# Widening steps moved behind the second layer, and the token transposes ahead of it, in the expert stage of a fused mLSTM, mixture-of-experts and MLP kernel

## The chip, the cores and the metric

The kernel runs on one core of a Trainium2 chip. The metric is the device time of one execution in microseconds (us), the median of several runs. The engines are named as the profile names them: PE (TensorE, matrix products), PEld (its weight loads), DVE (VectorE), ACT (ScalarE), POOL (GpSimd) and SP (SyncE, which issues most transfers here).

## What is computed

Three layers follow each other: a recurrent attention (mLSTM) over 4 sequences of 768 positions, a mixture of 8 experts of which each of the 3072 tokens uses one (`e_idx`, the largest of its 8 gate logits; `gate_w` is that gate's softmax), and a dense two-layer MLP. The expert layers are 320 -> 1024 -> 320, the MLP's 320 -> 2048 -> 320.

```python
def _moe_ref(x, w_gate, w_output_gate, w1, w2) -> np.ndarray:
...
    eom = 1.0 / (1.0 + np.exp(-(x @ w_output_gate)))
...
    for e in range(E):
        mask = e_idx == e
...
        h = np.maximum(x[mask] @ w1[e], 0.0)
        ye = h @ w2[e]
        out[mask] = gate_w[mask, None] * eom[mask, e, None] * ye
...
def _moe2_ref(x, w_in, w_out) -> np.ndarray:
    h = x @ w_in
    g = np.maximum(0.01 * h, h)
    return (g @ w_out).astype(np.float32)
```

The MLP's weights arrive as float64 and are rounded to float32 on the chip, from pairs of 32-bit words. That rounding is called widening here.

## The kernel before

Every large product is made in three parts: each operand is split into a rounded high part and a low part, and high times high, high times low and low times high are added up in one PSUM bank. PSUM has 8 banks that are given out in turn, so a new tile waits until the tile eight before it has been read.

After the attention, experts are worked on one after the other. Expert 0 is the first one; the others are ordered by falling token count and are called places 1 to 7. Places 1 to 3 have room for 512 tokens, places 4 to 7 for 384. One place does this:

- **First layer** (`Expert.one`, L989): 8 steps f = 0 to 7, each of 8 products (L954) into one PSUM tile `ph`, then `gh` by ACT (relu, L1004) and `gl` by DVE (what the rounding left, L1005).
- **Second layer** (`Expert.out`, L1008): one step per 128 tokens, 24 products each (L963 to L965: for every f two with `gh` and one with `gl`), then ACT scales the result (`yo`, L1019) and POOL writes it out by an indirect transfer (L1025).
- **Next tokens**: at f = 0 POOL issues the gathers of the next place's rows into `xr` (L978, one per 128 tokens); after f = 4 DVE copies the last 64 columns of them a second time (`dup`, L896); PE transposes them in three groups (`px`, L903, one group per 128 columns; the third group holds the copied columns), and ACT and DVE split them into `xh` and `xl` (L930 to L934).
- **Next weights**: seven parts are split, each by an ACT cast (`w1h`, `w2h`, L878) and a subtraction on DVE or POOL (`w1l`, `w2l`, L879). The loads of the weights after those are issued from SP when a raw buffer has been read (L783 to L791).
- **Widening**: a piece of 128 x 1024 numbers takes seven steps (L807 to L832): `size` (L809), `bound` (L813), `shift` (L816), `sign` (L819), `power` (L823) and `rest` (L827) on DVE, then `finish` (L831) on POOL and a transfer out. `rest` also lets ACT issue the load of a further piece. Places 1 to 3 do two pieces each, places 4 to 6 one, place 7 none; one more piece is done during the attention.

Within a stage the order of the instructions on PE, ACT, DVE and POOL is the order in which the program calls them. Two tables of closures set it (L1260 to L1284): `plan[f]` is called after step f of the first layer, `late[j]` after step j of the second. Before, `plan` holds the splits and the first four steps of the first piece, `late` the rest:

```python
for f in range(FE // P):
    gs.append(ex.one(wts[e], xs, f, e))
    ...
    for act in plan[f]:
        act()
for j in range(nj):
    ex.out(wts[e], gs, m, j, e)
    if j == 0 and tk:
        tk.turn()
        xs = tk.split()
    for act in late[j]:
        act()
```

Of the kernel before, what the change touches and what calls it, by code (L numbers as in the profile page):

```python
# [19 lines left out]
P = 128  # L20
# [34 lines left out]
def apart(tc, inst, before, why):  # L55
    """Writes of distinct rows of one tensor need not wait for each other."""
    for p in before:
        tc.declare_no_dep(inst.ins, p.ins, reason=why)
    before.append(inst)


def keep_warm(nc, psum, t, n):
    """Products nobody reads, so that the tensor engine's clock stays up over a wait."""
    pt = psum.tile([P, 512], F32, tag="ps", name="warm")
    for _ in range(n):
        nc.tensor.matmul(pt, t[:, 0:P], t[:, 0:512], start=True, stop=True)  # L66
# [8 lines left out]
def attention(ctx, tc, qT, kT, k, v, i_gate, f_gate, o_gate, psum, ident, router, side, feed, fill):  # L75
# [62 lines left out]

    # constants
    resetm = apool.tile([BH, NC_, P], F32, name="resetm")  # L140
# [4 lines left out]
    for j in range(3):  # L145
        nc.gpsimd.affine_select(
            sel, sel, pattern=[[-1, BH]], compare_op=ALU.not_equal, fill=1.0, base=-BH * j, channel_multiplier=1
        )
    # gate scans
    m = apool.tile([BH, S], F32, name="m")  # L150
# [8 lines left out]
    def gates(c0, c1, eng):  # L159
        """Steps that work out the gate factors of chunks c0 to c1 - 1."""  # L160
        n = c1 - c0
# [340 lines left out]
class Router:  # L502
# [54 lines left out]
    def clear(self):  # L557
        """Steps that give the slot table and the rows of xd that are written last their first contents."""
        put = self.nc.sync.dma_start
        late = lambda b: self.xd[b * S + (NC_ - 2) * P : (b + 1) * S].rearrange("(t p) e -> p t e", p=P)  # L560
        return [lambda: put(self.slots.rearrange("(p r) w -> p r w", p=P), self.init)] + [
            lambda b=b: put(late(b), self.zero[:, None, :].to_broadcast([P, 2, DM])) for b in range(B)
        ]
# [26 lines left out]
    def span(self, c, b):  # L590
        """Tiles routed together: a whole chunk, or one tile of the last chunk."""
        if c == NC_ - 1:
            return {B // 2 - 1: (0, B // 2), B - 1: (B // 2, B // 2)}.get(b, (0, 0))
        return (0, B) if b == B - 1 else (0, 0)
# [96 lines left out]
class Order:  # L691
    """Experts 1 to E - 1 in order of falling token counts, and the tiles of P slots past each one's share."""

# [32 lines left out]
    def expert(self):  # L726
        """Registers that hold the experts of places 1 to E - 1."""
        n = E - 1
        self.nc.gpsimd.tensor_copy(self.perm, self.key[:, 0:n])
        _, regs = self.nc.values_load_multi_w_load_instructions(  # L730
            self.perm[0:1, 0:n], engines=SP_ACT, min_val=1, max_val=n
        )
        return (0, *regs)

    def past(self, pool):
        """Steps that list the tiles of P slots past each expert's share."""
        v = self.nc.vector
# [57 lines left out]
def widen(nc, tile, dma, add, src, dst):  # L795
    """float64 bits (pairs of int32) rounded to float32, in small steps."""
    n = src.shape[1] // 2
    st = {}
    v = nc.vector

    def load():
        raw = tile("raw", 2 * n)
        dma.dma_start(raw, src)
        raw = raw.rearrange("p (n t) -> p n t", t=2)
        st["lo"], st["hi"] = raw[:, :, 0], raw[:, :, 1]

    def size():  # L807
        u = st["u"] = tile("u", n)
        v.tensor_scalar(u, st["hi"], 0x7FFFFFFF, None, ALU.bitwise_and)  # L809

    def bound():
        uf = st["u"].bitcast(F32)
        v.tensor_scalar(uf, uf, MIN64, MAX64, ALU.max, ALU.min)  # L813

    def shift():
        v.tensor_scalar(st["u"], st["u"], 3, (1 << 30) - 1, ALU.logical_shift_left, ALU.bitwise_and)  # L816

    def sign():
        v.scalar_tensor_tensor(st["u"], st["hi"], -(1 << 30), st["u"], ALU.bitwise_and, ALU.bitwise_or)  # L819

    def power():
        p = st["p"] = tile("p", n)
        v.tensor_scalar(p, st["u"], -(1 << 23), None, ALU.bitwise_and)  # L823

    def rest():
        r = st["r"] = tile("r", n).bitcast(F32)
        v.scalar_tensor_tensor(r, st["lo"].bitcast(U32), 2.0**-52, st["p"].bitcast(F32), ALU.mult, ALU.mult)  # L827

    def finish():
        uf = st["u"].bitcast(F32)  # L830
        add.tensor_add(uf, uf, st["r"])  # L831
        nc.sync.dma_start(dst, uf)  # L832

    return load, [size, bound, shift, sign, power, rest, finish]


class Weights:
    """One expert's weights as high and low parts, made in small steps."""

# [9 lines left out]
    def loads(self):  # L849
        """Steps that load both matrices, part by part."""  # L850
        a, b = self.src
        r1 = self.r1 = self.stage.tile([P, 3, FE], F32, tag="r1", name="r1")
        r2 = self.r2 = self.stage.tile([P, FE // P, DM], F32, tag="r2", name="r2")
        put = self.nc.sync.dma_start
        ones = [
            lambda: put(r1[:, 0], a[0:P]),
            lambda: put(r1[:, 1], a[P : 2 * P]),
            lambda: (put(r1[0:64, 2], a[2 * P :]), put(r1[64:P, 2], a[2 * P :])),
        ]
        b = b.rearrange("(f p) d -> p f d", p=P)  # L860
        return ones + [lambda f=slice(i, i + 2): put(r2[:, f], b[:, f]) for i in range(0, FE // P, 2)]

    def split1(self, t, eng):
        if t == 0:
            self.w1h = self.slot.tile([P, 3, FE], F32R, tag="w1h", name="w1h")
            self.w1l = self.slot.tile([P, 3, FE], F32R, tag="w1l", name="w1l")
        self.split(self.r1[:, t], self.w1h[:, t], self.w1l[:, t], eng)

    def split2(self, i, eng):
        nf = FE // P  # L870
        if i == 0:
            self.w2h = self.slot.tile([P, nf, DM], F32R, tag="w2h", name="w2h")
            self.w2l = self.slot.tile([P, nf, DM], F32R, tag="w2l", name="w2l")
        f = slice(2 * i, 2 * i + 2)
        self.split(self.r2[:, f], self.w2h[:, f], self.w2l[:, f], eng)

    def split(self, raw, hi, lo, eng):
        self.nc.scalar.copy(hi, raw)  # L878
        eng.tensor_sub(lo, raw, hi.bitcast(F32))  # L879

    def steps(self, engs):
# [5 lines left out]
class Tokens:  # L887
    """Token rows, turned to have features on the partitions and split in high and low parts."""

# [18 lines left out]
    def pieces(self):  # L908
        """Steps that turn the rows by blocks of 32 x 32 on the vector engine."""
        n, blocks = self.n, self.xr.rearrange("p j (g f) -> p j g f", f=32)  # L910
# [126 lines left out]
class Fill:  # L1037
    """The first slots of expert 0, worked on while the last tokens are routed."""

# [16 lines left out]
    def up(self, n):  # L1056
        """Products of n parts of the first layer."""
        for _ in range(n):
# [14 lines left out]
def overflow_tile(nc, pool, ex, slots, w1, w2, e, row):  # L1073
    """Tokens of expert e in the P slots from `row` on, all in float32."""
    psum, ident = ex.psum, ex.ident
# [27 lines left out]
def mlstm_moe_mlp(  # L1103
# [94 lines left out]
    with ExitStack() as mctx:  # L1198
# [19 lines left out]
        for e in range(E):  # L1218
# [25 lines left out]
            if e == 0:  # L1244
# [13 lines left out]
                ]  # L1258
            else:
                plan = [  # L1260
                    [w_(0, 0)],
                    [s1(nxt, 0, V)],
                    [s1(nxt, 1, G), w_(0, 1)],
                    [s1(nxt, 2, V), lambda: nx2.load1()],
                    [w_(0, 2), s2(nxt, 0, G), lambda: tk and tk.dup()],
                    [s2(nxt, 1, V)],
                    [s2(nxt, 2, G), w_(0, 3)],
                    [],
                ]
                late = [  # L1270
                    [s2(nxt, 3, V), lambda: nx2.load2(), w_(0, 4)],
                    [w_(0, 5, 6)],
                    [],
                    [],
                ]
                if nw == 2:
                    late[1] += [w_(1, 0, 1)]
                    late[2] += [w_(1, 2, 3, 4)]
                    late[3] += [w_(1, 5, 6)]
                if e < 4:  # L1280
                    late[1].append(past[e - 1])
                if e == E - 1:
                    plan[6], plan[7] = [s2(nxt, 2, G), s2(nxt, 3, V)], [lambda: nx2.load2()]
                    late = [[s1(nx2, 0, V)], [s1(nx2, 1, V)], [s1(nx2, 2, V)]]  # L1284
# [3 lines left out]
            for f in range(FE // P):  # L1288
# [3 lines left out]
                for act in plan[f]:  # L1292
                    act()
            for j in range(nj):
                ex.out(wts[e], gs, m, j, e)
                if j == 0 and tk:
                    tk.turn()
# [90 lines left out]
def _laid_out(inputs):  # L1388
    """q and k with positions innermost; k, v (and a one for each head) and o_gate as token rows of all heads."""
    import numpy as np  # L1390
# [35 lines left out]
```

## Time and profile before

| what | value |
|---|---|
| median of 3 runs | 796.43 us (796.18 to 798.04) |
| the profiled execution, first to last instruction | 798.3 us |
| PE busy in it | 745.3 us, 93% |
| DVE, POOL, ACT busy | 504.0 us, 383.1 us, 337.1 us |
| places 1 to 7 of the expert stage | 223.88 us to 440.68 us |

The profiled execution's span stands for its whole time; it lies 1.9 us above the median and 0.3 us above the slowest of the three runs. Busy time is a mean over stages with different limits; the expert stage has to be read by its own windows. A row of the timeline gives the start, the duration, the engine, the source line, the operation, what it writes and reads, and in brackets how long the engine had been idle and for what. Durations of instructions that follow each other overlap a little, because the next one starts before the last has drained.

### The profile page before, as it was taken

What the parts mean: (1) busy time and instruction counts of PE and PEld (TensorE: products, weight loads), DVE (VectorE), ACT (ScalarE), POOL (GpSimd) and SP (SyncE); (2) the same over time, 40 slices, a digit from 0 to 9 for tenths busy, and PEclk for the clock granted to TensorE, in tenths of its full rate; (3) what the DMA queues carried; (4) which work ended last, traced back from release to release, by engine and by line L of the source; (5) the groups of instructions that cost most, each with busy time, mean ns of one, the idle gap of its engine ahead of it and who ended that gap; (6) DMA issues with size and microseconds to landing.
All of it is one profiled execution on the core that took longest, in us unless ns stands there. A gap on an engine that the chain in (4) does not pass through costs nothing. (4 is left out here: it accounts for less than half of the span.)

```text
span 798.3 us, 14570 instructions
## 1 busy us (share of the span) xinstructions
PE 745.3 (93%) x5450; PEld 691.7 (87%) x5450; DVE 504.0 (63%) x956; ACT 337.1 (42%) x726; POOL 383.1 (48%) x408
## 2 busy tenths in 40 slices
PE   8778888899898998979989899999999999999998
PEld 6778888888788787978989898998998998998998
DVE  8889999977368988986575575606507417317120
ACT  5476545432353525334426535405416316226141
POOL 8556775554564836546535235506407307217131
PEclk9898897799998999889999999999999999999999
DMA  6885785410786655645655201100100100100000
GB/s 180 241 240 133 207 215 127 134 52 20 212 296 207 217 200 183 248 131 183 202 151 171 83 11 41 42 25 1 41 25 1 46 22 1 34 18 0 17 18 16
DMA packets 61790, 87.68 MB, mean 110 GB/s; under 512 B 8396, under 2 KB 53464, under 8 KB 60440
## 3 DMA queue, kind: packets, MB, share of 16 engines
q1 hardware_dynamic: 55928, 67.43, 28.6%
q10 hardware_dynamic: 2336, 10.75, 3.7%
q0 software_dynamic: 3456, 8.58, 3.4%
q8 instruction: 43, 0.70, 0.4%
q14 instruction: 27, 0.22, 0.1%
HBM read 67.87 MB, written 19.51 MB: 109 GB/s over the span
## 5 line engine op out<-in xcount | busy, mean ns | idle before, releaser
L1343 POOL TENSOR_TENSOR g2l<-lk,g2h 128x512 fp32r<-128x512 f32 (+1 forms) x112 | 126.7, 1134 | 213.8 <-ACT g2h L1342 203.7
L1352 DVE TENSOR_TENSOR lk<-p,lk 128x512 f32<-128x512 f32 (+1 forms) x112 | 69.0, 616 | 180.9 <-ACT lk L1351 179.0
L954 PE MATMUL p<-xhm,w1h 128*128 128x512 f32 (+1 forms) x336 | 119.7, 360 | 0.0
L954 PE MATMUL p<-xhm,w1l 128*128 128x512 f32 (+1 forms) x336 | 119.2, 359 | 0.0
L965 PE MATMUL po<-w2h,g2l 128*128 128x320 f32 x384 | 118.7, 309 | 0.0
L964 PE MATMUL po<-w2l,g2h 128*128 128x320 f32 x384 | 118.7, 309 | 0.0
L963 PE MATMUL po<-w2h,g2h 128*128 128x320 f32 x384 | 118.6, 309 | 0.0
L1351 ACT ACTIVATE lk<-p 128x512 f32<-128x512 f32 (+1 forms) x112 | 60.2, 538 | 73.5 <-PE p L954 73.5
L965 PE MATMUL po<-w2h,gl 128*128 128x320 f32 x208 | 69.8, 336 | 19.2 <-DVE gl L1005 19.2
L954 PE MATMUL p<-xlm,w1h 128*128 128x512 f32 (+1 forms) x224 | 80.6, 360 | 0.0
L963 PEld LDWEIGHTS po<-w2h,g2h 128*128 128x128 f32 x384 | 72.1, 188 | 0.2
L964 PEld LDWEIGHTS po<-w2l,g2h 128*128 128x128 f32 x384 | 72.1, 188 | 0.2
L965 PEld LDWEIGHTS po<-w2h,g2l 128*128 128x128 f32 x384 | 72.1, 188 | 0.0
L954 PEld LDWEIGHTS p<-xhm,w1h 128*128 128x128 f32 x336 | 63.6, 189 | 9.4 <-DVE xhm L934 0.2
L954 PEld LDWEIGHTS p<-xhm,w1l 128*128 128x128 f32 x336 | 63.4, 189 | 9.4
L963 PE MATMUL po<-w2h,gh 128*128 128x320 f32 x208 | 68.3, 328 | 0.0
L1025 POOL DMA_INDIRECT x<-yo,ms x26 | 28.1, 1080 | 80.9 <-ACT yo L1019 79.6
L964 PE MATMUL po<-w2l,gh 128*128 128x320 f32 x208 | 66.8, 321 | 0.0
L1366 ACT COPY yo<-po 128x320 f32<-128x320 f32 x24 | 10.2, 426 | 130.7 <-PE po L965 130.7
L965 PEld LDWEIGHTS po<-w2h,gl 128*128 128x128 f32 x208 | 41.8, 201 | 24.9 <-DVE gl L1005 24.9
L1342 ACT CAST g2h<-lk 128x512 fp32r<-128x512 f32 (+1 forms) x112 | 61.7, 551 | 1.6 <-DVE lk L1352 1.6
L916 DVE STREAM_TRANSPOSE xtm<-x2r 32x384 f32<-32x384 f32 (+3 forms) x144 | 59.6, 414 | 2.8
(245 smaller groups left out, 1703.7 us busy)
## 6 DMA issues: line engine op xcount, KB each, us to landing
r<-in_moe_w_dram SPq DMA_DIRECT2D x6, 1280.0 KB
r<-in_moe_w_dram SPq DMA_DIRECT2D x7, 1024.0 KB
raw<-in_moe_w_out_dram ACTq DMA_DIRECT2D x5, 1024.0 KB
r<-in_moe_w_dram SPq DMA_DIRECT2D x16, 256.0 KB
raw<-in_moe_w_in_dram ACTq DMA_DIRECT2D x4, 1024.0 KB
v<-in_v_dram SPq DMA_DIRECT2D x24, 164.0 KB
o<-in_o_gate_dram SPq DMA_DIRECT2D x6, 640.0 KB
k<-in_k_dram SPq DMA_DIRECT2D x24, 160.0 KB
```

Of the source, the lines that this page charges most:

```text
L916: self.nc.vector.transpose(out=xt[f, k].rearrange("p k (j t) -> p k j t", t=P)[:, :, :, t], in_=blocks[t, :, g].rearrange("p j k f -> p k ...
L954: nc.tensor.matmul(ps, a, b, start=(i == 0), stop=(i == len(seq) - 1))
L963: nc.tensor.matmul(ps, gh[:, js], wh, start=(f == 0), stop=False)
L964: nc.tensor.matmul(ps, gh[:, js], wl, start=False, stop=False)
L965: nc.tensor.matmul(ps, gl[:, js], wh, start=False, stop=(f == n - 1))
L1025: put = self.nc.gpsimd.indirect_dma_start(out=self.x2, out_offset=bass.IndirectOffsetOnAxis(ap=ms[:, j, 1:2], axis=0), in_=yo, in_offset=None,
L1342: nc.scalar.copy(gh, lk)
L1343: nc.gpsimd.tensor_sub(gl, lk, gh.bitcast(F32))
L1351: nc.scalar.activation(lk, pf, AF.Copy, scale=0.01)
L1352: nc.vector.tensor_max(lk, pf, lk)
L1366: nc.scalar.copy(yo, po[:, :DM])
```

## The change

In the places 1 to 7 the following moves or changes:

- The ACT cast of each weight part is called one step ahead of its subtraction (`high1`, `high2` and `low1`, `low2` take the place of `split1`, `split2`).
- Of the widening, `size` is now an ACT instruction (absolute value of the high word read as float32), `bound` a POOL instruction. That holds for the piece in the attention too.
- `size` of the first piece is called at f = 0, `bound` at f = 7; all that follows, and the whole second piece, is called in the second layer.
- The fourth part of `w2l` and the next load of `w2` move from the first step of the second layer to f = 7.
- `turn` and `split` of the next tokens are called ahead of the second layer, not after its first step (expert 0 keeps its order).

```diff
 def size():
     u = st["u"] = tile("u", n)
-    v.tensor_scalar(u, st["hi"], 0x7FFFFFFF, None, ALU.bitwise_and)
+    nc.scalar.activation(u.bitcast(F32), st["hi"].bitcast(F32), AF.Abs)
 def bound():
     uf = st["u"].bitcast(F32)
-    v.tensor_scalar(uf, uf, MIN64, MAX64, ALU.max, ALU.min)
+    nc.gpsimd.tensor_scalar(uf, uf, MAX64, MIN64, ALU.min, ALU.max)
...
+h1, h2, l1, l2 = nxt.high1, nxt.high2, nxt.low1, nxt.low2
 plan = [
-    [w_(0, 0)],
-    [s1(nxt, 0, V)],
-    [s1(nxt, 1, G), w_(0, 1)],
-    [s1(nxt, 2, V), lambda: nx2.load1()],
-    [w_(0, 2), s2(nxt, 0, G), lambda: tk and tk.dup()],
-    [s2(nxt, 1, V)],
-    [s2(nxt, 2, G), w_(0, 3)],
-    [],
+    [lambda: h1(0), w_(0, 0)],
+    [lambda: l1(0, V), lambda: h1(1)],
+    [lambda: l1(1, G), lambda: h1(2)],
+    [lambda: l1(2, V), lambda: h2(0), lambda: nx2.load1()],
+    [lambda: l2(0, G), lambda: h2(1), lambda: tk and tk.dup()],
+    [lambda: l2(1, V), lambda: h2(2)],
+    [lambda: l2(2, G), lambda: h2(3)],
+    [w_(0, 1), lambda: l2(3, V), lambda: nx2.load2()],
 ]
 late = [
-    [s2(nxt, 3, V), lambda: nx2.load2(), w_(0, 4)],
-    [w_(0, 5, 6)],
-    [],
-    [],
+    [w_(0, 2), w_(1, 0)],
+    [w_(0, 3, 4), w_(1, 1)],
+    [w_(0, 5, 6), w_(1, 2)],
+    [w_(1, 3, 4, 5, 6)],
 ]
-if nw == 2:
-    late[1] += [w_(1, 0, 1)]
-    late[2] += [w_(1, 2, 3, 4)]
-    late[3] += [w_(1, 5, 6)]
...
+if e and tk:
+    tk.turn()
+    xs = tk.split()
 for j in range(nj):
     ex.out(wts[e], gs, m, j, e)
-    if j == 0 and tk:
+    if e == 0 and j == 0:
         tk.turn()
         xs = tk.split()
```

How the order on two engines changes is shown at three places. The first is DVE at place 5, from step f = 3 of the first layer on; `xr` are the gathered rows of the next tokens, `u` is the widening's piece, `w1l` and `w2l` are low parts of the next weights. Before:

```order
L813 TENSOR_SCALAR u<-u 128x1024
L1005 SCALAR_TENSOR_TENSOR gl_3_4787<-ph_3_4777,gh_3_4786 128x384
L879 TENSOR_TENSOR w1l<-r_4532,w1h 128x1024
L1005 SCALAR_TENSOR_TENSOR gl_4_4806<-ph_4_4796,gh_4_4805 128x384
L816 TENSOR_SCALAR u<-u 128x1024
L896 COPY xr_4738<-xr_4738 128x3x64
L1005 SCALAR_TENSOR_TENSOR gl_5_4825<-ph_5_4815,gh_5_4824 128x384
L879 TENSOR_TENSOR w2l<-r_4652,w2h 128x640
L1005 SCALAR_TENSOR_TENSOR gl_6_4840<-ph_6_4830,gh_6_4839 128x384
L819 SCALAR_TENSOR_TENSOR u<-raw,u 128x1024
L1005 SCALAR_TENSOR_TENSOR gl_7_4856<-ph_7_4846,gh_7_4855 128x384
```

With the change, the same place:

```order
L1026 SCALAR_TENSOR_TENSOR gl_3_4787<-ph_3_4777,gh_3_4786 128x384
L892 TENSOR_TENSOR w1l<-r_4534,w1h 128x1024
L1026 SCALAR_TENSOR_TENSOR gl_4_4808<-ph_4_4798,gh_4_4807 128x384
L917 COPY xr_4738<-xr_4738 128x3x64
L1026 SCALAR_TENSOR_TENSOR gl_5_4824<-ph_5_4814,gh_5_4823 128x384
L892 TENSOR_TENSOR w2l<-r_4599,w2h 128x640
L1026 SCALAR_TENSOR_TENSOR gl_6_4839<-ph_6_4829,gh_6_4838 128x384
L1026 SCALAR_TENSOR_TENSOR gl_7_4854<-ph_7_4844,gh_7_4853 128x384
L892 TENSOR_TENSOR w2l<-r_4599,w2h 128x640
L953 TENSOR_TENSOR xl_4874<-px_0_4861,xh_4873 128x384
```

The four steps on `u` have left this stretch; the copy of `xr` still stands between `gl_4` and `gl_5`, and the split of the next tokens follows `gl_7`.

The second place is POOL from the second layer of place 5 to the first of place 6 (`yo` are results that are written out, `x_79` is where to). Before:

```order
L1025 DMA x_79<-yo_0_4884,ms 3072x320
L1024 MEMSET gap_91 1x1
L1025 DMA x_79<-yo_1_4941,ms 3072x320
L831 TENSOR_TENSOR u<-u,r 128x1024
L1024 MEMSET gap_91 1x1
L1025 DMA x_79<-yo_2_4976,ms 3072x320
L1286 TENSOR_LOAD total
L978 DMA xr_5009<-xd,ms 128x320 x3
```

With the change:

```order
L1046 DMA x_79<-yo_1_4938,ms 3072x320
L1045 MEMSET gap_91 1x1
L1046 DMA x_79<-yo_2_4972,ms 3072x320
L831 TENSOR_TENSOR u<-u,r 128x1024
L1304 TENSOR_LOAD total
L999 DMA xr_5009<-xd,ms 128x320 x3
```

`finish` (L831) now stands between the last result of a place and the gathers of the next one.

The third place is POOL in the first layer of place 6, from its gathers on, with the change (before, the row of L813 is not on this engine):

```order
L999 DMA xr_5009<-xd,ms 128x320 x3
L892 TENSOR_TENSOR w1l<-r_4794,w1h 128x1024
L892 TENSOR_TENSOR w2l<-r_4859,w2h 128x640 x2
L813 TENSOR_SCALAR u<-u 128x1024
L1045 MEMSET gap_91 1x1
```

`bound` has joined the three subtractions that follow the gathers.

## Rows read from the trace of the kernel before

**Rows 1.** The page, part 1: busy time of each engine, share, instructions.
```profile
PE 745.3 (93%) x5450; PEld 691.7 (87%) x5450; DVE 504.0 (63%) x956; ACT 337.1 (42%) x726; POOL 383.1 (48%) x408
```

**Rows 2.** Waits of PE, 238 to 420 us, then 373 to 392 us: us, times, longest.
```profile
PE po L965 <- DVE gl L1005: 17.9, 20, 3.1
...
PE po L965 <- DVE gl L1005: 3.0, 4, 1.0
```

**Rows 3.** Windows: second layers of places 1 to 7: us, busy by engine, PEclk, DMA.
```profile
238.81:260.85 22.04, 19.21 (x109) 18.13 (x108) 18.20 (x28) 7.42 (x13) 9.21 (x11) 0.85 0.62 214
275.78:296.29 20.51, 17.83 (x110) 17.02 (x109) 17.71 (x23) 4.57 (x8) 8.68 (x10) 0.92 0.62 207
311.20:331.98 20.78, 18.72 (x107) 17.91 (x105) 18.33 (x26) 4.25 (x8) 8.19 (x9) 0.84 0.70 232
343.28:362.79 19.51, 15.01 (x82) 14.21 (x82) 12.82 (x13) 3.61 (x7) 8.62 (x8) 0.83 0.56 183
373.88:391.06 17.18, 14.22 (x83) 13.17 (x82) 11.58 (x16) 3.61 (x7) 5.16 (x6) 0.90 0.57 180
402.15:419.02 16.87, 13.98 (x83) 12.91 (x82) 11.51 (x16) 3.62 (x7) 5.17 (x6) 0.90 0.62 176
430.12:440.68 10.56, 10.56 (x74) 10.56 (x73) 5.44 (x6) 3.98 (x6) 4.00 (x6) 1.00 0.97 286
```

**Rows 4.** Timeline of PE: the 12 transposes in expert 0.
```profile
218.49 0.49 PE L903 MATMUL px<-ident,xr 128*128 128x128 f32 x3
219.31 1.20 PE L903 MATMUL px<-ident,xr 128*128 128x128 f32 x9 [0.32 <-DMA xr<-xd,ms]
```

**Rows 5.** Timeline of DVE in the first layers of places 4 and 5.
```profile
341.90 6.41 DVE L816 TENSOR_SCALAR u<-u 128x1024 int32<-128x1024 int32 x1
...
367.28 1.23 DVE L879 TENSOR_TENSOR w1l<-r,w1h 128x1024 fp32r<-128x1024 f32 x1 [0.38 <-issue]
...
368.89 4.96 DVE L813 TENSOR_SCALAR u<-u 128x1024 f32<-128x1024 f32 x1
...
374.24 2.35 DVE L879 TENSOR_TENSOR w1l<-r,w1h 128x1024 fp32r<-128x1024 f32 x1
376.52 0.55 DVE L1005 SCALAR_TENSOR_TENSOR gl<-ph,gh 128x384 fp32r<-128x384 f32 x1
376.99 0.68 DVE L816 TENSOR_SCALAR u<-u 128x1024 int32<-128x1024 int32 x1
377.59 0.28 DVE L896 COPY xr<-xr 128x192 f32<-128x192 f32 x1
```

**Rows 6.** Timeline of POOL: subtractions at places 2 to 4, last write, gathers, subtractions at place 5.
```profile
272.60 2.42 POOL L879 TENSOR_TENSOR w1l<-r,w1h 128x1024 fp32r<-128x1024 f32 x1
...
306.41 2.42 POOL L879 TENSOR_TENSOR w1l<-r,w1h 128x1024 fp32r<-128x1024 f32 x1
...
342.34 2.42 POOL L879 TENSOR_TENSOR w1l<-r,w1h 128x1024 fp32r<-128x1024 f32 x1
344.71 3.04 POOL L879 TENSOR_TENSOR w2l<-r,w2h 128x640 fp32r<-128x640 f32 x2
...
363.95 1.00 POOL L1025 DMA_INDIRECT x<-yo,ms  x1 [0.18 <-issue]
365.25 0.99 POOL L978 DMA_INDIRECT xr<-xd,ms  x1 [0.30 <-issue]
...
369.36 2.41 POOL L879 TENSOR_TENSOR w1l<-r,w1h 128x1024 fp32r<-128x1024 f32 x1
371.72 1.57 POOL L879 TENSOR_TENSOR w2l<-r,w2h 128x640 fp32r<-128x640 f32 x1
```

**Rows 7.** Timeline of ACT in the first layer of place 1: casts of the next weights.
```profile
234.27 1.05 ACT L878 CAST w1h<-r 128x1024 fp32r<-128x1024 f32 x1
...
239.71 0.74 ACT L878 CAST w2h<-r 128x640 fp32r<-128x640 f32 x1 [3.90 <-DMA r<-in_moe_w_dram]
```

**Rows 8.** Line L288, a POOL instruction with one input: ns min/median/max, first and last start.
```profile
L288 POOL TENSOR_SCALAR_AFFINE_SELECT pe<-pe x24: 1089/1102/1542, 11.9 to 172.4; 128x1024 f32<-128x1024 f32 x24
```

More of the change, by code (lines that the diff above doesn't have):

```diff
@@ L861, in loads, with part1, part2, high1 @@
         return ones + [lambda f=slice(i, i + 2): put(r2[:, f], b[:, f]) for i in range(0, FE // P, 2)]
-    def split1(self, t, eng):
+    def part1(self, t):
+        return self.r1[:, t], self.w1h[:, t], self.w1l[:, t]
+    def part2(self, i):
+        f = slice(2 * i, 2 * i + 2)
+        return self.r2[:, f], self.w2h[:, f], self.w2l[:, f]
+    def high1(self, t):
         if t == 0:
@@ L866, in split1, with high2 @@
             self.w1l = self.slot.tile([P, 3, FE], F32R, tag="w1l", name="w1l")
-        self.split(self.r1[:, t], self.w1h[:, t], self.w1l[:, t], eng)
-    def split2(self, i, eng):
+        raw, hi, _ = self.part1(t)
+        self.nc.scalar.copy(hi, raw)
+    def high2(self, i):
         nf = FE // P
@@ L873, in split2, with low1, low2, low @@
             self.w2l = self.slot.tile([P, nf, DM], F32R, tag="w2l", name="w2l")
-        f = slice(2 * i, 2 * i + 2)
-        self.split(self.r2[:, f], self.w2h[:, f], self.w2l[:, f], eng)
-    def split(self, raw, hi, lo, eng):
+        raw, hi, _ = self.part2(i)
         self.nc.scalar.copy(hi, raw)
-        eng.tensor_sub(lo, raw, hi.bitcast(F32))
+    def low1(self, t, eng):
+        self.low(*self.part1(t), eng)
+    def low2(self, i, eng):
+        self.low(*self.part2(i), eng)
+    def low(self, raw, hi, lo, eng):
+        eng.tensor_sub(lo, raw, hi.bitcast(F32))
+    def split1(self, t, eng):
+        self.high1(t)
+        self.low1(t, eng)
+    def split2(self, i, eng):
+        self.high2(i)
+        self.low2(i, eng)
     def steps(self, engs):
@@ L1282, in mlstm_moe_mlp @@
                 if e == E - 1:
-                    plan[6], plan[7] = [s2(nxt, 2, G), s2(nxt, 3, V)], [lambda: nx2.load2()]
+                    plan[7] = [lambda: l2(3, V), lambda: nx2.load2()]
                     late = [[s1(nx2, 0, V)], [s1(nx2, 1, V)], [s1(nx2, 2, V)]]
```

## The prediction

> **What bounds the kernel now.** I read the busy times first: PE is busy for 93% of the span, DVE for 63%, POOL for 48% [rows 1]. Where PE is nearly always busy, only what makes it wait or run slowly is to be had. The change touches places 1 to 7, so I then read the waits of PE and one window for each second layer.
>
> PE has one wait of size there: the low products wait for `gl`, which DVE still owes when the second layer begins, 17.9 us in 20 waits [rows 2]. The windows [rows 3] give each second layer, the transposes in it included; what lies between two of them is a first layer: 14.93 us from 260.85 to 275.78 at place 2, 14.91 and 11.30 at places 3 and 4, 11.09 at places 5 and 6. Place 7, with three steps, no transposes and the clock at 1.00, takes 10.56 us, so a step without losses is 3.52 us. A transpose adds (1.20 - 0.49) / 6 = 0.12 us [rows 4]; 12 of them add 1.42, 9 add 1.06. Without losses a second layer would be 4 x 3.52 + 1.42 = 15.50 us (places 1, 2), 15.14 (place 3, which turns 384 tokens) and 11.62 (places 4 to 6). The six windows lie above that by 6.54, 5.01, 5.64, 7.89, 5.56 and 5.25, in all **35.9 us**. 17.9 of it are the waits. The other 18.0 go with the granted clock, which is 0.83 to 0.92 in these windows against 1.00 at place 7: after the waits it falls from 2.4 to 1.2 GHz for some us. At place 5 that part is 5.56 - 3.0 [rows 2, 3] = 2.6 us.
>
> The reader should next see why DVE is late. Its mask step L816 takes 0.68 us at 376.99, but 6.41 at 341.90; L813 takes 4.96 at 368.89 [rows 5]. Over the first of these POOL runs `w1l` and two `w2l`, from 342.34 to 347.75 [rows 6], and L816 ends 0.6 us later, its own time. So such a step stands still while POOL works, through several POOL instructions in a row. `gl`, which reads PSUM, keeps its 0.55 us.
>
> **The change, part by part.** *The waits for `gl`.* With the widening steps gone DVE has in a first layer eight `gl` of 0.55, two `w1l` of 1.23 [rows 5], two `w2l` of 5/8 the size, so 0.8 each, and the copy of 0.28: less than 9 us of work in 11 to 15. I take all 17.9 us as gone.
>
> *A new wait.* The transposes now stand between the two layers on PE, and their third group reads the columns that DVE's copy makes. The copy stands behind `gl_4` in DVE's queue; it has one input in SBUF, as the mask step has, so I take it to stand still through POOL's chain `w1l`, `w2l`, `w2l` and the new `bound`. The first three take 2.42 + 3.04 = 5.46 us [rows 6]. `bound` on POOL the trace doesn't have: from below it is the one-input instruction of the same shape, 1.10 us [rows 8], from above the two-input `w1l`, 2.42 [rows 6]; it has one input, so I take 1.10. The chain is 6.5 us, the copy 0.28 behind it.
>
> With times counted from the start of a first layer:
> - Place 2: POOL's `w1l` starts at 272.60 - 260.85 = 11.75 [rows 3, 6], the copy ends at 18.5. PE has done its first layer and two groups at 14.93 + 0.95 = 15.9. Wait 2.6 us.
> - Place 3: `w1l` at 10.12, the copy ends at 16.9, PE is there at 14.91 + 0.71 = 15.6. Wait 1.3.
> - Place 4: `w1l` at 10.36, copy 17.15, PE at 12.0. Wait 5.1.
> - Places 5 and 6: before, `finish` ran ahead of the last result; now it stands between that and the gathers (the second order above). The last write ends at 364.95 - 362.79 = 2.2 [rows 3, 6], `finish`, of `w1l`'s kind, adds 2.4, three gathers 4.1 (365.25 to 369.36), so `w1l` starts at 8.8, the chain ends at 15.3, the copy at 15.6. PE is there at 11.8. Wait 3.8 each.
> - Place 1: ACT's cast of `w2h` waits 3.90 us for its load, until 239.71 [rows 7]. It is called a step earlier now, so four `gh` stand behind it instead of three, then `gl_4`, and the copy meets POOL's `w2l`: it ends about 242.4. PE is there at 238.81 + 0.95. Wait 2.6.
>
> That is 19.2 us. From above, DVE's second `w1l` (1.2) and `gl_4` (0.5) come out of the chain ahead of the copy as well, 1.7 us more each at places 2 to 6: 27.9. At places 5 and 6 that `w1l` is ready at about 7.9, ahead of the chain, so I keep the low value there; at places 2 to 4 its order against the chain is open and I take the middle: 3.5, 2.2, 6.0. With 3.8 twice and 2.6 the wait is **21.9 us**.
>
> *The half clock.* Each place still has a long wait of PE ahead of 10 us of products. I keep 2.6 us per place, as at place 5, where the waits (3.0) are nearest in size to the forecast ones: 6 x 2.6 = 15.6. The mean over the places, 3.0, gives 18.0.
>
> *Covered edits.* `size` on ACT is one pass over 128 x 1024, as the cast of 1.05 us [rows 7]; ACT is busy 42%. The piece in the attention gains some 1.4 us on DVE and loses 1.1 on POOL: between -1 and +1 on the end, taken as 0. The fourth `w2l` part and the load of `w2` come a step earlier, `load1` waits for a `w1l` that is some 2 us later; those loads have most of a place to land, so 0, at most +2. The raw loads follow `rest`, 3.5 us later, and the MLP's own stage is far off: 0. Place 7 only changes the order of casts.
>
> *Sum.* Before: 35.9. After: 21.9 + 15.6 = 37.5. The difference is +1.6 us. From the profiled execution's 798.3 us that is 799.9; it lies 1.9 above the median, so the **forecast** is 796.4 + 1.6 = **798.0 us**. Its own bounds: 19.2 + 15.6 - 35.9 = -1.1 and 27.9 + 18.0 - 35.9 = +10, so 795 to 806.
>
> **The rivals.** *Slip (faster).* The copy gets in between two POOL instructions, or DVE reaches it before the chain starts. Then the third group is ready with the others, and six small losses for the transposes' handover stay, about 1.5 each (half of the 3.0): 9 in place of 35.9, so -27 and 769 us; with slips at half of the places 783 to 787. For it: at 374.24 DVE's `w1l` got away with 2.35 instead of 1.23, beside a chain with a gap in it. Against it: L816 and L813 were held over two and three POOL instructions [rows 5, 6]. 0.17. The Trainium skill ("SBUF — State Buffer", section "SBUF: two separate sides") calls the port that the two engines share an exclusive lock, held for the whole instruction, on which the loser fully blocks. The trace agrees on the blocking, 6.41 against 0.68 us; who gets the lock next the page leaves open, and if it were given up after each instruction to the one waiting, the copy would follow `w1l` and the time would be this rival's 769 us. The rows speak against that.
>
> *Dear `bound` (slower).* `bound` runs at 2.42 us: +1.32 at places 2 to 6 is 6.6, and the second pieces in the second layers of places 1 to 3 hold up DVE's splits for some 3 more: 798.0 + 6.6, up to 808 us. It decides from about 1.5 us per step on. For it, every 128x1024 POOL row in the expert stage is 2.4 us; against it, those have two inputs. 0.15.
>
> *Spill (slower).* What left the first layer doesn't fit in the second. At places 1 to 3 DVE does two pieces there, each two steps of 0.68 and two of 1.23 [rows 5], 7.6 us in all, and three splits of 0.55; POOL does a `bound` and a `finish` while DVE's steps stand still (1.1 + 2.4), and the second `finish` (2.4) comes behind all of it: 15.2 us, where only 4 x 3.52 = 14.1 are left behind the transposes. The last `finish`, the gathers, the chain and the copy then come 1.1 us later, up to 2 with what else DVE has there, at places 2 to 4: some +5, 803 us. It decides where `finish` ends later in the next first layer than it does today. Against it: the raw loads and the writes leave gaps on both engines. 0.13.
>
> *Small gain.* One or two of the waits above are shorter, or the clock holds at two places: 785 to 793 us. 0.05.
>
> **How the numbers follow.** The forecast case has 0.50. About 2.4 us (0.3%) is what a measurement can tell from no change. Within the case's bounds I give 0.09 to faster than that, 0.28 to within it, 0.13 to slower. With the rivals: faster 0.09 + 0.17 + 0.05 = 0.31, same 0.28, slower 0.13 + 0.15 + 0.13 = 0.41. The forecast case's own range is 795 to 806. The whole range leaves out most of the slip (0.14) and the far end of the slow cases (0.06): 787 to 810.
>
> **What would show it.** Right: no waits of PE for `gl` from 238 to 420 us, six for the copied `xr` at the third `px` group, 21.9 us in all, the longest at place 4; the copy on DVE stretched to several us and ending just behind `bound`; `bound` near 1.1; the granted clock of the second-layer windows still below 1.00. Wrong: a copy of 0.28 us in every place and a clock near 1.00 (slip); `bound` near 2.4; `finish` starting more than 4 us into the next first layer at places 2 to 4 (spill). A time under 787 would mean that the copy isn't held as the mask step was.

## The result and the profile after

The changed kernel takes **776.38 us** (median; 775.62 to 780.95) against 797.23 us of the kernel before, measured beside it; the ratio is 0.9743, with a 95% interval of 0.9712 to 0.9774. That is 20.9 us faster, where 798.0 us (787 to 810) had been forecast. The profiled execution spans 773.8 us.

The page's part 1, and the waits of PE from 220 to 420 us (total, times, longest); they answer to [rows 1, 2]:

```profile
PE 731.2 (95%) x5450; PEld 682.2 (88%) x5450; DVE 472.4 (61%) x936; ACT 343.1 (44%) x736; POOL 399.8 (52%) x418
...
PE px L924 <- DVE xr L917: 8.1, 3, 4.1
PE px L924 <- DMA xr<-xd,ms: 0.5, 1, 0.5
```

No wait for `gl` is left. The third group of transposes does wait for the copied rows, as forecast, but at three places instead of six, and 8.1 us instead of 21.9. The windows of the second layers of places 1 to 7 (us, busy time by engine, PEclk, DMA share, GB/s) answer to [rows 3]:

```profile
236.64:252.95 16.31, 15.61 (x109) 15.37 (x108) 15.29 (x26) 7.82 (x14) 11.39 (x12) 1.00 0.68 206
267.88:289.14 21.26, 17.15 (x109) 16.91 (x108) 18.34 (x24) 4.78 (x8) 9.80 (x11) 0.92 0.59 184
304.08:324.20 20.12, 16.83 (x106) 16.60 (x105) 17.01 (x24) 4.46 (x8) 8.32 (x10) 0.92 0.62 192
335.82:348.34 12.52, 12.01 (x81) 11.62 (x82) 9.79 (x13) 3.73 (x9) 10.00 (x9) 1.00 0.82 244
359.44:370.98 11.54, 11.54 (x82) 11.54 (x81) 9.62 (x13) 2.68 (x6) 8.06 (x8) 1.00 0.91 274
382.28:393.83 11.55, 11.55 (x83) 11.54 (x81) 9.42 (x12) 2.69 (x6) 7.59 (x8) 1.00 0.93 253
404.93:415.49 10.56, 10.56 (x74) 10.56 (x73) 4.16 (x5) 3.53 (x5) 3.51 (x6) 1.00 0.97 282
```

Against the lengths without losses (15.50, 15.50, 15.14 and three times 11.62 us) the six windows now lose 0.81, 5.76, 4.98, 0.90, -0.08 and -0.07 us: **12.3 us** in place of 35.9. Places 2 and 3 hold nearly all of it, and only there does the clock show less than 1.00. The whole stretch of places 1 to 7 went from 216.80 to 193.78 us. The other 1.5 of the 24.5 us between the two profiled spans lie elsewhere; the start of place 1 alone scatters from 221.0 to 226.2 us over the profiled executions below, so I compare windows, not spans, for what happens at a place.

The question is why places 2 and 3 went as forecast and places 4 to 6 not. The timelines of DVE and POOL (start, us, engine, line, operation) at place 2:

```profile
264.24 7.94 DVE L892 TENSOR_TENSOR w1l<-r,w1h 128x1024 fp32r<-128x1024 f32 x1
...
272.69 0.28 DVE L917 COPY xr<-xr 128x256 f32<-128x256 f32 x1
...
263.71 0.95 POOL L999 DMA_INDIRECT xr<-xd,ms  x1 [0.30 <-issue]
264.68 2.40 POOL L892 TENSOR_TENSOR w1l<-r,w1h 128x1024 fp32r<-128x1024 f32 x1
267.03 3.05 POOL L892 TENSOR_TENSOR w2l<-r,w2h 128x640 fp32r<-128x640 f32 x2
270.06 1.03 POOL L813 TENSOR_SCALAR u<-u 128x1024 f32<-128x1024 f32 x1
```

and at place 5:

```profile
355.93 1.22 DVE L892 TENSOR_TENSOR w1l<-r,w1h 128x1024 fp32r<-128x1024 f32 x1
357.07 0.55 DVE L1026 SCALAR_TENSOR_TENSOR gl<-ph,gh 128x384 fp32r<-128x384 f32 x1
358.79 0.78 DVE L917 COPY xr<-xr 128x192 f32<-128x192 f32 x1 [1.18 <-DMA xr<-xd,ms]
...
359.95 1.66 DVE L892 TENSOR_TENSOR w2l<-r,w2h 128x640 fp32r<-128x640 f32 x1
...
355.63 0.95 POOL L999 DMA_INDIRECT xr<-xd,ms  x1 [0.30 <-issue]
356.60 2.82 POOL L892 TENSOR_TENSOR w1l<-r,w1h 128x1024 fp32r<-128x1024 f32 x1
359.37 3.68 POOL L892 TENSOR_TENSOR w2l<-r,w2h 128x640 fp32r<-128x640 f32 x2
363.03 1.61 POOL L813 TENSOR_SCALAR u<-u 128x1024 f32<-128x1024 f32 x1
```

At place 2 DVE's `w1l` stands from 264.24 through all four POOL steps to 272.18, and the copy waits behind it. At place 5 the copy meets the same chain in the middle of POOL's `w1l` and is through at 359.57, 0.15 us after that one step: it slipped in, and POOL's `w2l` pair is longer (3.68 against 3.05) because DVE's `w2l` got in there again. So the same step is held over a chain in one place and let in after one instruction in the other.

### The profile page after: what moved, and what is told of

Its sections match the earlier page's. It is cut to its first block, busy times and chain, and to the rows that moved or that the text cites. A ratio compares the mean times of both kernels' runs of the same rounds, so it can differ in the third digit from the quotient of the medians.

```text
span 773.8 us, 14577 instructions
## 1 busy us (share of the span) xinstructions
PE 731.2 (95%) x5450; PEld 682.2 (88%) x5450; DVE 472.4 (61%) x936; ACT 343.1 (44%) x736; POOL 399.8 (52%) x418
## 4 chain that ended last, share of the span: by engine, by line
PE 62%; DMA 11%; DVE 10%; issue 8%; POOL 7%; ACT 1%; SPq 0%; POOLq 0%; DVEq 0%; ACTq 0%
PE p L975 23%; PE po L984 9%; PE po L986 9%; PE po L985 9%; DMA xr<-xd,ms 6%; PE ph L975 4%; PE psc L313 3%; DMA r<-in_moe_w_dram 3%; DVE y L390 2%; DVE ww L320 2%; POOL x L1046 2%; PE ppv L369 1%; DMA o<-in_o_gate_dram 1%; POOL w2l L892 1%; POOL xr L999 1%
## 5 line engine op out<-in xcount | busy, mean ns | idle before, releaser
L984 PE MATMUL po<-w2h,gh 128*128 128x320 f32 x208 | 66.2, 318 | 0.0
L986 PE MATMUL po<-w2h,gl 128*128 128x320 f32 x208 | 65.7, 316 | 0.1
L975 PE MATMUL ph<-xh,w1l 128*128 128x384 f32 (+1 forms) x168 | 60.8, 362 | 0.0
L975 PE MATMUL ph<-xh,w1h 128*128 128x384 f32 (+1 forms) x168 | 60.8, 362 | 0.0
```

The costliest lines, as they stand in the source:

```text
L975: nc.tensor.matmul(ps, a, b, start=(i == 0), stop=(i == len(seq) - 1))
L984: nc.tensor.matmul(ps, gh[:, js], wh, start=(f == 0), stop=False)
L986: nc.tensor.matmul(ps, gl[:, js], wh, start=False, stop=(f == n - 1))
```

## The experiments

### What holds a DVE step, measured by itself

The first theory was that the moment of arrival decides: what comes up just ahead of the chain is held, what comes up inside it is let in. A kernel of blocks, each like this (`hi` is written by ACT at the start of a block, so both engines start together; `wait` grows from block to block):

```python
if gather:
    nc.gpsimd.indirect_dma_start(out=rows, out_offset=None, in_=src, in_offset=...)
for i in range(3):
    nc.gpsimd.tensor_sub(low[:, i * 1024 : (i + 1) * 1024], ra, rb)
...
    nc.vector.scalar_tensor_tensor(spare[:, 0:n], pf[:, 0:n], 0.0, hi[:, 0:n], ALU.max, ALU.subtract)
...
    nc.vector.tensor_copy(cpy[:, 0:192], pa[:, 0:192])
```

> This kernel computes none of the three layers; it is 80 small blocks. In each, POOL runs three subtractions of 128x1024 back to back (with one gather ahead of them in half of the blocks), and DVE, after products that read PSUM and take from 0.1 to 5 us, runs one probe: a copy of 128x192 or a two-input subtraction of 128x1024. Theory 1 (it depends on the arrival): a probe that comes up in the last half us ahead of the first subtraction is held to the end of all three, some 7.5 us; one that comes up while a subtraction runs is let in when that one ends, so it takes at most 2.4 us more than its own time, copy and subtraction alike. Theory 2 (the chain decides): every probe is held to the end of the third subtraction whenever it comes. Theory 3 (the kind decides): the copy is let in at the next end, the two-input subtraction is held to the end of the chain.

Two blocks of it, one with a gather ahead and one without:

```profile
54.00 0.96 POOL L90 DMA_INDIRECT rows<-in_k_dram,ids  x1 [0.77 <-ACT ids L85]
54.98 6.93 POOL L94 TENSOR_TENSOR low<-ra,rb 128x1024 f32<-128x1024 f32 x3
...
55.55 6.49 DVE L101 COPY cpy<-pa 128x192 f32<-128x192 f32 x1
...
226.05 6.96 POOL L94 TENSOR_TENSOR low<-ra,rb 128x1024 f32<-128x1024 f32 x3 [1.16 <-ACT ra L88]
...
227.11 1.40 DVE L101 COPY cpy<-pa 128x192 f32<-128x192 f32 x1
```

With the gather ahead the copy is up 0.57 us into the chain and ends 0.13 us after the end of the third subtraction; without it, up 1.06 us into the chain, it is through after the first. All 40 blocks of each sort agree, copy and subtraction alike, wherever in the chain the probe came up (one block with a gather is left out, where the chain itself started late). Both sorts of block begin with a wait of POOL for ACT (0.77 and 1.16 us in the rows shown), so the gather is what differs. None of the three theories holds as put: **behind a gather** POOL's whole run holds DVE off, **without one** only the instruction that DVE meets.

The next run asked what ends that hold: in turn nothing, a running DVE step, a one-word fill on POOL, a wait of POOL's first or second subtraction for ACT, and an indirect write in place of the gather.

> Like the run with the 80 blocks, again none of the three layers: 60 blocks, always an indirect transfer of POOL first, then three subtractions of 128x1024 on POOL, and a copy on DVE that comes up at one of ten moments. Six kinds: plain; a two-input DVE subtraction already running when POOL's first one comes up; a one-word fill on POOL between transfer and chain; a wait of the first subtraction for ACT; a wait of the second one for ACT; an indirect write in place of the gather. Theory A (POOL keeps the port from the transfer on until it has to wait): plain, fill and write hold the copy to the end of the third subtraction; the running DVE subtraction and a wait ahead of the chain let it in at the end of the subtraction it meets; with a wait in the middle it gets in at that wait and after it. Theory B (any other instruction behind the transfer ends it): as A, but the fill lets the copy in as well. Theory C (a copy behind DVE's own late start is let in by chance): no pattern by kind.

| kind, 10 blocks each | copy ends |
|---|---|
| plain; fill; indirect write | at the end of the third subtraction (9, 10 and 10 blocks; plain's first block started late) |
| first subtraction waits for ACT | at once in the gap, then at the end of the subtraction that it meets (10 of 10) |
| second subtraction waits for ACT | at the end of the first one, then as above (10 of 10) |
| DVE step meant to be running | that step, up 0.43 us behind the gather's start, was itself held to the end of the chain (10 of 10) |

Two of its blocks, with the fill and with the wait at the head:

```profile
252.78 0.09 POOL L102 MEMSET gap<- 1x8 f32 x1
252.84 6.92 POOL L110 TENSOR_TENSOR low<-ra,rb 128x1024 f32<-128x1024 f32 x3
...
253.88 6.01 DVE L119 COPY cpy<-pa 128x192 f32<-128x192 f32 x1
...
363.20 6.95 POOL L110 TENSOR_TENSOR low<-ra,rb 128x1024 f32<-128x1024 f32 x3 [1.25 <-ACT ra L105]
...
364.51 1.15 DVE L119 COPY cpy<-pa 128x192 f32<-128x192 f32 x1
```

Theory A holds for the fill, the write and both waits. The kind with the running step did not make what it was meant to, so a third kernel moved a DVE subtraction in steps of some 0.07 us across the last of two gathers, with a copy behind it that comes up inside the chain:

> None of the three layers: 28 blocks, each with two gathers of POOL and behind them three subtractions of 128x1024; on DVE one two-input subtraction that comes up later from block to block (from the first gather to the chain), products that read PSUM, and then a copy that comes up while the chain runs. Theory A (POOL keeps the port from the gather on until it has to wait): where the DVE subtraction gets the port ahead of the chain and still runs when POOL's first subtraction comes up, POOL waits for it and the copy is let in at the end of a subtraction; in the other blocks the copy stands to the end of the third. The border should lie where it lies in the expert stage, with a start some 0.3 to 0.5 us behind that of the last gather. Theory C (chance): no such border.

Two neighbouring blocks on either side of the border:

```profile
165.07 0.95 POOL L105 DMA_INDIRECT rows<-in_k_dram,ids  x1 [0.30 <-issue]
166.04 7.37 POOL L107 TENSOR_TENSOR low<-ra,rb 128x1024 f32<-128x1024 f32 x3
...
165.38 1.22 DVE L109 TENSOR_TENSOR plow<-pa,pb 128x1024 f32<-128x1024 f32 x1
...
167.84 1.08 DVE L111 COPY cpy<-pa 128x192 f32<-128x192 f32 x1
...
175.36 0.95 POOL L105 DMA_INDIRECT rows<-in_k_dram,ids  x1 [0.31 <-issue]
176.33 6.93 POOL L107 TENSOR_TENSOR low<-ra,rb 128x1024 f32<-128x1024 f32 x3
...
175.93 8.42 DVE L109 TENSOR_TENSOR plow<-pa,pb 128x1024 f32<-128x1024 f32 x1
```

A subtraction up 0.31 us behind the last gather's start runs in its 1.22 us, the chain is 0.44 us longer (7.37 against 6.93: POOL waited for it), and the copy behind it is let in after the first subtraction. Up 0.57 us behind, it is held for 8.42 us. Of 27 blocks (the first, where the chain itself started late, is left out), the six from -0.02 to +0.31 us let the copy in; in the eight earlier ones (-0.75 to -0.09) the last gather is late, the subtraction is over when the chain comes up, and the copy is held to the end; in the thirteen later ones the subtraction is. The expert stage fits: at places 4, 5 and 6 DVE's `w1l` comes 0.30, 0.30 and 0.31 us after the last gather's start (355.93 - 355.63 at place 5) and POOL's `w1l` takes 2.8 us, at places 2 and 3 it comes 0.53 and 0.52 us after (264.24 - 263.71) and is held.

### The same in the kernel

One call moved, at places 5 and 6 alone: DVE's second `w1l` behind the copy, so that it no longer runs when the chain comes up.

```diff
+if e in (5, 6):
+    plan[3] = [lambda: h2(0)]
+    plan[4] = [lambda: l2(0, G), lambda: h2(1), lambda: tk.dup(), lambda: l1(2, V), lambda: nx2.load1()]
```

> The changed kernel, where at places 5 and 6 alone DVE's second w1l is called behind the copy of the gathered rows. Theory A: that w1l no longer runs when POOL's chain comes up, so nothing makes POOL wait, and the copy, up in the middle of POOL's w1l, is held to the end of the chain as at places 2 and 3: a wait of PE of 3 to 3.8 us in both places and some 1.6 us at the half clock behind each, 783 to 788. If places 5 and 6 are spared for another reason (fewer tokens, the copy being short): no change, 774 to 778.

It took 786.60 us (0.9855 of before, 0.983 to 0.988). Place 5:

```profile
357.94 0.95 POOL L999 DMA_INDIRECT xr<-xd,ms  x1 [0.30 <-issue]
358.90 2.41 POOL L892 TENSOR_TENSOR w1l<-r,w1h 128x1024 fp32r<-128x1024 f32 x1
361.27 3.04 POOL L892 TENSOR_TENSOR w2l<-r,w2h 128x640 fp32r<-128x640 f32 x2
364.27 1.04 POOL L813 TENSOR_SCALAR u<-u 128x1024 f32<-128x1024 f32 x1
...
360.95 4.51 DVE L917 COPY xr<-xr 128x192 f32<-128x192 f32 x1 [1.63 <-DMA xr<-xd,ms]
...
361.73:378.00 16.27, 13.30 (x83) 13.06 (x81) 13.05 (x14) 2.78 (x6) 6.69 (x8) 0.90 0.63 195
```

The copy is now held from 360.95 to the end of `bound`, and the second layer loses 4.65 us (16.27 - 11.62) at a clock of 0.90, at place 6 4.62. Theory A has it. So some ten us of the change's gain (786.60 against 776.38) hang on 0.2 us of timing between DVE and a gather (0.31 us behind it against 0.53).

The same move at places 2 and 3 had been run before the rule was known:

> At places 2 and 3 alone DVE's second low part of w1 is called behind the copy of the gathered rows, not ahead of it. Theory 1 (arrival): the copy now comes up while POOL's w1l runs and is let in at its end, about 267.5 and 302.5 us on the changed kernel's scale, ahead of PE (268.9 and 304.9). The two waits of 4.1 and 3.3 us go, and about 1.65 us at the half clock behind each with them: 776.4 - 10.7, so 764 to 769. Theory 2 (chain): the copy is held to the end of the chain as the subtraction was, the waits stay: 774 to 779.

772.99 us (0.9703; 0.9677 to 0.9729). Theory 2's mechanism was right and its time was not: the copy was held, 4.61 us at place 2, but it stood in front of the chain's end without the subtraction and a `gl` ahead of it, so the two waits fell, to 2.40 and 2.14 us, and the windows' losses to 2.52 and 3.84. At place 2 the clock stayed at 1.00, at place 3 it did not:

```profile
268.26:286.28 18.02, 15.62 (x110) 15.38 (x109) 17.79 (x22) 4.76 (x8) 9.32 (x11) 1.00 0.61 184
301.21:320.19 18.98, 16.84 (x107) 16.60 (x106) 18.64 (x23) 4.77 (x9) 8.51 (x11) 0.91 0.62 192
```

A one-word fill behind the gathers (`nc.gpsimd.memset(self.gap, 0)` at the end of `gather`):

> The changed kernel with a one-word fill on POOL behind the gathers of each place. Theory B: the fill ends the hold, DVE's second w1l at places 2 and 3 gets in at the latest at the end of POOL's w1l, the copy follows by 270 and 305 us, and the waits of 4.1 and 3.3 us shrink to 1.5 at most, the half clock with them: 766 to 771. Theory A: nothing changes, 774 to 779.

776.23 us (0.9724; 0.9699 to 0.9749), three waits for the copy of 7.7 us in all: no change, as theory A has it. Then a wait at the head of the chain, at places 2 and 3:

```diff
+if e in (2, 3):
+    plan[1:6] = [
+        [lambda: l1(0, V), lambda: h1(2)],
+        [lambda: h2(0)],
+        [lambda: l1(2, V), lambda: h2(1)],
+        [lambda: h1(1), lambda: l1(1, G), lambda: l2(0, G), lambda: tk.dup()],
+        [lambda: nx2.load1(), lambda: l2(1, V), lambda: h2(2)],
+    ]
```

> The changed kernel, where at places 2 and 3 alone the ACT cast of the second part of w1 and POOL's subtraction of it are called at f = 4, so that POOL's chain begins with a wait for ACT of about 1 us behind the gathers. Theory A: the wait ends POOL's hold, DVE's second w1l gets in at the end of the gathers, the copy at the end of POOL's w1l, about where PE comes for it; the two waits (4.1 and 3.3 us) and the half clock behind them (1.65 and 1.7) go: 764 to 769. If the hold has nothing to do with POOL's waiting: the chain only starts 1 us later, 776 to 780.

**769.77 us** (0.9641; 0.9617 to 0.9665), the fastest of the series. Place 3, and the windows of places 2 to 4:

```profile
301.10 2.41 POOL L892 TENSOR_TENSOR w1l<-r,w1h 128x1024 fp32r<-128x1024 f32 x1 [2.00 <-ACT w1h L875]
303.46 3.68 POOL L892 TENSOR_TENSOR w2l<-r,w2h 128x640 fp32r<-128x640 f32 x2
...
302.36 1.29 DVE L917 COPY xr<-xr 128x192 f32<-128x192 f32 x1 [0.94 <-DMA xr<-xd,ms]
...
271.84:288.12 16.28, 15.62 (x110) 15.38 (x109) 16.05 (x21) 4.75 (x8) 10.82 (x11) 1.00 0.69 206
303.04:318.18 15.14, 15.14 (x107) 15.05 (x106) 14.84 (x21) 4.57 (x9) 11.69 (x12) 1.00 0.73 219
331.07:344.05 12.98, 12.23 (x82) 11.62 (x83) 10.20 (x14) 4.15 (x9) 10.50 (x9) 1.00 0.76 242
```

POOL waits 2.00 us for ACT's cast, and the copy, up inside `w1l`, is through 0.14 us after its end. The losses of places 2 and 3 fall from 10.74 to 0.78 us. Some 1.7 us of that come back at place 4: the gathers start 7.5 us into the place instead of 6.6, PE waits 1.6 us for the gathered rows ahead of the first transpose, and the window loses 1.36 us instead of 0.90. Places 1 to 7 take 184.80 us, 9.0 less than in the changed kernel, but the medians differ by 6.6 only, so that the time lies just above the 764 to 769. Place 1 starts at 226.2 us in this execution and at 221.7 in that of the changed kernel; why that start scatters was not looked into. A further version tried to mend that: `finish` of the second piece behind the next place's gathers, and the wait at the head at f = 6 in places 2 to 4.

> The wait ahead of POOL's chain at places 2 to 4 (cast of the second part of w1 and POOL's three subtractions called at f = 6), and the finish step of the second piece called behind the next place's gathers at places 1 to 3. Theory A: the hold is broken as before, and at place 4 the gathers come 2.4 us earlier, so that the waits for the gathered rows there (2.6 us in all in the run with the wait at places 2 and 3) go, some 0.8 us of place 2 with them: 769.8 - 3, so 765 to 769. If finish behind the gathers lengthens the hold over the copy: 772 or more.

775.72 us (0.9713; 0.968 to 0.9745), a miss. The gathers at place 4 do start earlier, 4.8 us into the place instead of 7.5, but their rows still land late, which stays open; PE waits 0.96 and 1.60 us for them and 1.59 us for the copy there, and the window loses 6.0 us at a clock of 0.81. The rival's time came out, but not its mechanism: the copy was let in at the end of POOL's `w1l`. What `finish` behind the gathers held was DVE's first `w1l`, for 3.12 us. The changed kernel beside it:

> The changed kernel as it is, on the same chip and beside the run above: 774 to 779 by every theory, and the same places waited at (2 and 3, some 3 to 4 us each for the copied rows), none at 5 and 6.

775.76 us (0.972; 0.9692 to 0.9749), with waits of 7.7 us for the copy and losses of 6.79 and 4.45 us at places 2 and 3, none at 5 and 6.

### Which part of the change earned it

> The kernel before with the transposes ahead of the second layer and nothing else. If the moved widening steps earn the gain: DVE's backlog stays, the copy behind it holds the third group of transposes and takes over part of the waits for gl: 792 to 802. If the transposes' new place earns a good part: 787 or less.

> The changed kernel with the transposes back behind the first step of the second layer. If the moved widening steps earn the gain: DVE is still held at places 2 and 3, now PE waits for gl there, some 3 us each, nothing at places 4 to 6: 774 to 780. If the transposes' new place earns a good part of it: waits at the second step come back in each place, 783 or more.

> The changed kernel with size and bound back on DVE. If the hold behind the gathers is the whole story of places 2 and 3: the chain there is 1.03 us shorter, the two waits shrink by that much each, and DVE has 1.4 us more per piece where it has room: 772 to 777. If the move to ACT and POOL earns part of the gain: 780 to 786.

Losses of the six second layers are worked out as above, from each kernel's windows:

| kernel | us | ratio to before | losses, us | waits of PE in it, us | clock, us at most |
|---|---|---|---|---|---|
| before | 797.23 | 1 | 35.9 | 17.9 for `gl` | 15.0 |
| transposes ahead, nothing else | 785.85 | 0.9857 | 23.1 | 14.3 copy, 1.1 rows, 0.5 `gl` | 8.8 |
| changed, `size` and `bound` on DVE | 783.07 | 0.9829 | 18.0 | 12.2 copy, 0.6 rows | 5.2 |
| changed, transposes behind the first step | 778.45 | 0.9785 | 17.6 | 9.2 for `gl` | 6.8 |
| changed | 776.38 | 0.9743 | 12.3 | 8.1 copy, 0.5 rows | 3.3 |
| changed, wait at the head at places 2, 3 | 769.77 | 0.9641 | 2.3 | 0.8 copy, 0.6 rows | 0 |

Each ratio is to the kernel before measured beside that run. The last column is (1 - clock) x length, summed over the six windows; where PE waits at the lower clock, it counts the same time as the column before.

The transposes alone give 1.4% and the moved steps alone 2.2% of a change of 2.6%, so they overlap: DVE's backlog has to be waited for once (transposes ahead), or not be there (steps moved). Once the steps are moved, what the transposes' place adds shows in the losses, 17.6 against 12.3 us, but the times don't tell it from nothing (0.9751 to 0.9819 and 0.9712 to 0.9774). For the transposes alone the rival expectation came true. They hardly shorten the waits, 17.9 to 15.9 us, but make one or two of several at each place, and what the windows lose beside the waits falls from 18.0 to 7.2 us; the clock's column falls with it, from 15.0 to 8.8. With the transposes back, 778.45 us is within what was expected, though places 1 and 4 lose 4.02 and 4.64 us as well, which was not. With `size` and `bound` on DVE the rival expectation came true again (783.07 us), by the same rule: place 3 loses nothing, since DVE's `w1l` comes up 0.02 us after the last gather's start there (298.30 against 298.28), but places 4 to 6 lose 5.09, 4.59 and 4.59 us; at place 5 `w1l` comes up 0.28 us ahead of the last gather (353.97 against 354.25), is over before the chain starts at 356.02, and the copy is held 3.44 us. So moving those two steps earns its share more through DVE's timing against the gathers than through the 1.4 us of work.

## Why the prediction was wrong

- *The waits for `gl` go.* Right: none is left.
- *A new wait for the copy.* The mechanism was right at places 2 and 3: 4.11 and 3.29 us against a forecast of 3.5 and 2.2 with upper bounds of 4.3 and 3.0 (1.7 above 2.6 and 1.3), so near the upper bound or past it, because DVE's second `w1l` was held ahead of the copy. **The step that failed is "I take it to stand still through POOL's chain", applied to every place.** At places 4 to 6 it forecast 13.6 us and PE waited 0.5, for rows. The runs put in its place: POOL's run behind an indirect transfer holds DVE off to its end, unless POOL has to wait in it; at places 4 to 6 it had to (its `w1l` took 2.8 us instead of 2.4), for a DVE step that came 0.3 us behind the last gather's start. The mask steps of [rows 5] that I generalised from were held behind gathers (of place 4's the last row is below, place 5's are in [rows 6]). The one that got away, 2.35 us at 374.24, met a POOL step that had waited 0.65 us for ACT, the second row below; I had read it as an exception.

```profile
340.34 1.99 POOL L978 DMA_INDIRECT xr<-xd,ms  x1 [0.30 <-issue]
...
373.94 1.58 POOL L879 TENSOR_TENSOR w2l<-r,w2h 128x640 fp32r<-128x640 f32 x1 [0.65 <-ACT w2h L878]
```

- *Place 1.* Forecast 2.6, measured 0.7: its chain waits for ACT's casts (1.76 us ahead of `w1l`, 1.49 ahead of the first `w2l`), so the copy (0.65 us) was held by one `w2l` only, and the load of `w2` made ACT wait 1.94 us instead of 3.90 [rows 7].
- *The half clock, 15.6 us.* Mis-sized: beside the waits, places 2 and 3 lost 5.76 - 4.11 = 1.65 and 4.98 - 3.29 = 1.69 us, which is what the clock took there ((1 - 0.92) x 21.26 = 1.7 and (1 - 0.92) x 20.12 = 1.6), and the other places kept 1.00. The 2.6 of place 5 before was put down to the clock as a whole, but by [rows 3] the clock took (1 - 0.90) x 17.18 = 1.7 at most. The other 0.9 lay neither in the waits nor in the clock; what it was stays open. In all six places it was at most 15.0 of the 18.0. The length of a wait does not decide the clock's part by itself: with the copy moved first, a wait of 2.40 us at place 2 left it at 1.00, and one of 2.14 at place 3 went with 0.91.
- *`bound` on POOL.* Right: 1.03 to 1.08 us where DVE doesn't come between; up to 1.66 where it does. The rival with 2.42 fell.
- *Spill.* It was there and cost little: `finish` of the second piece starts 4.4, 4.1 and 4.0 us into the first layers of places 2 to 4, about the 4 us that I had named as its mark, but no wait for `gl` came of it, and place 4 paid 0.5 us for late rows.
- *Sum.* Two sums of the forecast are off in the last digit (8.7 for 8.8 and 27.7 for 27.9), which changes nothing. 37.5 us of losses forecast, 12.3 measured. Of the 25.2 between them, 20.7 lie at places 4 to 6 (21.4 forecast, 0.75 measured) and 4.4 at place 1; at places 2 and 3, 10.9 were forecast and 10.74 measured, which is luck: the waits there were 1.7 us longer than forecast (7.4 for 5.7) and the half clock 1.9 us less (3.3 for 5.2). The rival named *slip* was what happened at four places of six, and the time lies between what it gave for half of the places ("783 to 787") and for all (769); its chance of 0.17 was too low because what decides it had not been looked for in the rows.

The Trainium skill ("SBUF — State Buffer", section "SBUF: two separate sides") has the port that DVE and POOL share as an exclusive lock, held for the whole instruction. The blocks without a gather agree: a copy of 0.25 us takes at most 2.38. The blocks with one show a hold over three instructions, 6.9 us, and there the measurement decides.

## What to carry to other kernels

A step that shares a port with another engine must be costed by what precedes that engine's run, not by the run's length alone: look for every earlier instance, held or let in, and find what tells them apart before using the mean. Where POOL issues indirect transfers and then a run of tensor steps, let the run begin with a wait (a late input), which gave 6.6 us here, or keep what the bound engine needs ahead of the gathers, which was not run. And one merged wait of TensorE can cost less than several small ones of nearly the same sum: with the transposes alone moved, 15.9 us of waits went with 7.2 us of other losses, before the change 17.9 with 18.0.

## What the runs showed of the hardware

- Behind an indirect transfer, gather or write, POOL's tensor instructions hold off DVE's copies, mask steps and two-input steps in SBUF until POOL has to wait: three subtractions, 6.9 us, in all 39 blocks with a plain gather of the first kernel and all 39 plain, fill, write and late-subtraction blocks of the second. `gl`, which reads PSUM, kept its 0.55 us. A one-word fill between doesn't end the hold (10 of 10); a wait for ACT of 1.25 us, in the kernel of 2.00, does, for the rest of the run.
- A DVE subtraction that comes up between 0.02 us ahead of the last gather's start and 0.31 us behind it still runs when POOL's first subtraction comes up, goes first and ends the hold (6 of 6 blocks). One that comes up from 0.42 us on is held; between 0.31 and 0.42 us nothing was measured. One that comes up 0.09 to 0.75 us ahead of the gather delays that gather, which then takes 1.29 to 1.95 us instead of 0.95, and the hold stays (8 of 8). Why POOL keeps the port over instructions was not shown.
- The copy of 128x192 takes 0.25 us by itself; where it was held or met an instruction, it ended 0.12 to 0.18 us behind the end of what it waited for.
